# Attention weights of batches 3 to 7 transposed through DRAM and VectorE instead of TensorE, in a pooled-attention and FFN kernel

## The chip, the cores and the metric

The kernel runs on one NeuronCore of a Trainium2 chip. A core has TensorE (in the profile PE for matmuls, PEld for the loads of their stationary operand), VectorE (DVE), ScalarE (ACT), GpSimd (POOL), SyncE (SP, which only issues DMAs here) and 16 DMA engines. Each engine has its own queue and works through it in order; semaphores tie them together. The metric is the device time of one execution in microseconds (us).

## The reference

```python
# B, H, S, D = 8, 8, 576, 64; Sp = 72 pooled keys
k_p = k.reshape(B, H, Sp, 8, D).mean(axis=3)
v_p = v.reshape(B, H, Sp, 8, D).mean(axis=3)
scores = matmul(q, k_p.transpose(0, 1, 3, 2)) / sqrt(D)
attn = exp(scores - scores.max(-1, keepdims=True))
attn = attn / (attn.sum(-1, keepdims=True) + 1e-09)
x = matmul(attn, v_p).transpose(0, 2, 1, 3).reshape(B * S, H * D)   # 4608 x 512
h = x @ w_in                                                         # 512 x 2048
out = maximum(0.01 * h, h) @ w_out                                   # 2048 x 512
```

All is float32. The FFN matmuls and attention times V are done in a rounded format (F32R) with each operand split into a high and a low part, and three products hi*hi, hi*lo, lo*hi.

## The kernel before

**FFN.** The 4608 rows of x are worked through in nine chunks of 512, the first one in two halves, so there are ten stretches. In a stretch, each of 16 blocks of d_ff has an `m1` (12 matmuls into `ph`, lines 677 to 679, then Prelu, the cast `gh` and the remainder `gl`) and, two blocks behind, an `m2` (12 matmuls into the four accumulators `acc`, lines 701 to 703). `ph` has two PSUM banks.

**Attention.** A batch has five tiles of q rows: four of 128 and one of 64, in two pieces (three in batches 0 and 2). Its heads go in two groups of four (g = 0, 1), so a batch has ten units of tile and group. A unit goes through these steps:
- `q_unit`: q comes from DRAM in 16 small DMAs with its 32x32 blocks in place, and VectorE transposes the blocks (line 380); from batch 1 on.
- `s_unit` (`sa`): two matmuls give the scores `pss` (line 409), VectorE takes the negated maximum (417), ScalarE the exponentials with their sums (419).
- `norm_unit` (`sb`): VectorE adds 1e-9 and takes the reciprocal (430, 431), GpSimd writes `at`, the normalised weights, in two products (433, 437): keys 0 to 63 of the heads in pairs, and the last 8 keys of each head four times over.
- `p_unit` (`pu`): TensorE transposes `at` in three 128-column matmuls into the PSUM tile `pp` (line 458); ScalarE copies `pT` hi and rem from it (460, 461), VectorE writes the low parts (464, 468).
- `av_unit` (`au`), once for each piece and group: 8 matmuls `pa` (483 to 486) from `pT` and the pooled V, then x hi and lo (500, 501). There is one set of `pT` for both groups.

**Order.** TensorE's order is written out by hand: a list of attention steps (`line_up`) is spread evenly over the beats of a stretch, two beats per `m1` or `m2`, and reaches its end four beats before the stretch does. A stretch takes the pieces that make the next chunk. The order on the other engines comes from a planner that simulates the program; it is fixed at run time. From batch 1 on, `pss`, `pp`, `pa`, `pk`, `pv` share two PSUM banks. The pool `three` has three buffers for `at`, `outs` three for `o`.

Of the kernel before, what the change touches and what calls it, by code (L numbers as in the profile page):

```python
# [10 lines left out]
F32 = mybir.dt.float32  # L11
# [4 lines left out]
ALU = mybir.AluOpType  # L16
# [8 lines left out]
def tile_pooled_attention_ffn(  # L25
# [9 lines left out]
    nc = tc.nc  # L35

    P = 128
# [3 lines left out]
    MAIN = 64  # L41
    REM = SP - MAIN
# [13 lines left out]
    PIECES = [  # L56
        [[(0, 128), (128, 128)], [(256, 128), (384, 128)], [(512, 64)]],
        WHOLE,
        [[(0, 128), (128, 128)], [(256, 128)], [(384, 128), (512, 64)]],
        [[(0, 128), (128, 128), (256, 64)], [(320, 128), (448, 128)]],  # L60
        WHOLE,
        WHOLE, WHOLE, WHOLE,
    ]
# [4 lines left out]
    )  # L68
    TAIL_STEPS = "pu40 au20 pu41 au21"
    SPLIT = 8  # L70
    KSCALE = 1.0 / (POOL * 8.0)

# [133 lines left out]
    def bank(b, name):  # L206
        nonlocal turn
        pool, tag = banks[turn % len(banks)] if b == 0 else banks[0]
        turn += 1
        return pool.tile([P, NK, P], F32, tag=tag, name=name)  # L210
# [216 lines left out]
    def norm_unit(b, t, g, e, sm):  # L427
        n = tiles[b][t][1]
        eng = nc.vector if b == 0 and t in NORM_DVE else nc.gpsimd
        nc.vector.tensor_scalar_add(sm[:n], sm[:n], 1e-9)  # L430
        nc.vector.reciprocal(sm[:n], sm[:n])  # L431
        at = wide(b, t, g, "at", [3, P]) if wide_at(b, t, "at") else three.tile([P, 3, P], F32, tag="at", name=f"at{b}_{t}_{g}")
        eng.tensor_tensor(  # L433
            at[:n, 0:2, :].rearrange("a i (h s) -> a (i h) s", h=2), e[:n, :, 0:MAIN],
            sm[:n].unsqueeze(2).broadcast_to([n, 4, MAIN]), op=ALU.mult,
        )
        ins = eng.tensor_tensor(
            at[:n, 2, :].rearrange("a (h c s) -> a h c s", h=4, c=4),
            e[:n, :, MAIN:].unsqueeze(2).broadcast_to([n, 4, 4, REM]),
            sm[:n].unsqueeze(2).unsqueeze(3).broadcast_to([n, 4, 4, REM]), op=ALU.mult,  # L440
        )
        if b == 0:
            anchor[eng] = ins
        return at

    def piece_tiles(b, j, g):
        if b > 0 or g == 0 or j == 2:
            return pT
        return {
            part: spare(10 - n // 2, n % 2, t.shape, F32R, f"pT_{part}{b}_{j}_{g}")  # L450
            for n, (part, t) in enumerate(pT.items())
        }

    def p_unit(b, t, g, at, pc, o):
        n = tiles[b][t][1]
        pp = bank(b, f"pp{b}_{t}_{g}")
        for i in range(3):
            nc.tensor.transpose(pp[:, i, :n], at[:n, i, :], ident[:n, :n])  # L458
        rem = pc["rem"][:, o : o + n]
        nc.scalar.copy(pc["hi"][:, :, o : o + n], pp[:, 0:2, :n])  # L460
        ins = nc.scalar.copy(rem, pp[:, 2, :n])
        if b == 0:
            anchor["act"] = ins
        nc.vector.tensor_tensor(
            pc["lo"][:, :, o : o + n], pp[:, 0:2, :n], pc["hi"][:, :, o : o + n].bitcast(F32),
            op=ALU.subtract,
        )
        nc.vector.scalar_tensor_tensor(
            rem, pp[:, 2, :n], m_lo, rem.bitcast(F32), op0=ALU.mult, op1=ALU.subtract
        )  # L470
# [59 lines left out]
    def attention(b):  # L530

        st = {}
        where = [(j, sum(n for _, n in piece[:i]))
                 for j, piece in enumerate(PIECES[b]) for i in range(len(piece))]

        def loads():
            (start_k, st["k"]), (start_v, st["v"]) = load_k(b), load_v(b)
            start_k()
            q_of[b, 0] = load_q(b, 0)
            q_of[b, 1] = load_q(b, 1)  # L540
            start_v()
            for t in range(2, 5):
                q_of[b, t] = load_q(b, t)

        def loads1():
            (start_k, st["k"]), (start_v, st["v"]) = load_k(b), load_v(b)
            start_k()
            start_v()

        def lk():  # L550
            st["ks"] = load_k(b)[1]() if b > 1 else st["k"]()

        def lv():
            st["vs"] = load_v(b)[1]() if b > 1 else st["v"]()

        def ku():
            place_k(b, *st["ks"])

        def vu():
            place_v(b, *st["vs"])  # L560

        def qu(t):
            def f():
                st["qT", t] = q_unit(b, t, q_of[b, t])
                after = every.index((b, t)) + 2
                if after < len(every) and every[after] not in q_of:
                    q_of[every[after]] = load_q(*every[after])
            return f

        def sa(t, g):  # L570
            def f():
                st["e", t, g] = s_unit(b, t, g, st["qT", t])
            return f

        def sb(t, g):
            def f():
                st["at", t, g] = norm_unit(b, t, g, *st["e", t, g])
            return f

        def pu(t, g):  # L580
            def f():
                j, o = where[t]
                if (j, g) not in st:
                    st[j, g] = piece_tiles(b, j, g)
                p_unit(b, t, g, st["at", t, g], st[j, g], o)
            return f

        def au(j, g):
            def f():
                av_unit(b, j, g, st[j, g])  # L590
            return f

        return {
            "loads": loads1 if b else loads, "lk": lk, "lv": lv, "ku": ku, "vu": vu,
            **{f"q{t}": qu(t) for t in range(len(where))},
            **{f"{n}{t}{g}": u(t, g) for n, u in (("sa", sa), ("sb", sb), ("pu", pu))
               for t in range(len(where)) for g in range(2)},
            **{f"au{j}{g}": au(j, g) for j in range(len(PIECES[b])) for g in range(2)},
        }

    def line_up(pieces):

        flat = [(b, j, t) for b, j in pieces for t in range(len(tiles[b]))
                if tiles[b][t] in PIECES[b][j]]
        out = []

        def add(b, u):
            out.append((b, u))

        fresh = {}  # L610
        for n, (b, j, t) in enumerate(flat):
            nxt = flat[n + 1] if n + 1 < len(flat) else None
            first = n == 0 or flat[n - 1][:2] != (b, j)
            last = nxt is None or nxt[:2] != (b, j)
            if n == 0:
                if t == 0:
                    add(b, "ku")
                add(b, f"q{t}")
            if (b, t) not in fresh:
                add(b, f"sa{t}0")  # L620
            if not first:
                add(b, f"pu{t - 1}0")
            if (b, t) not in fresh:
                add(b, f"sb{t}0")
            if nxt:
                add(nxt[0], f"q{nxt[2]}")
            add(b, f"sa{t}1")
            if n == 0 and t == 0:
                add(b, "vu")
            if last:  # L630
                if not first:
                    add(b, f"pu{t}0")
                    add(b, f"sb{t}1")
                else:
                    add(b, f"sb{t}1")
                    if nxt and nxt[0] == b:
                        add(b, f"sa{nxt[2]}0")
                        fresh[nxt[0], nxt[2]] = 1
                    add(b, f"pu{t}0")
                if nxt and nxt[0] == b and (nxt[0], nxt[2]) not in fresh:  # L640
                    add(b, f"sa{nxt[2]}0")
                    fresh[nxt[0], nxt[2]] = 1
                if nxt and nxt[0] != b:
                    add(nxt[0], "ku")
                add(b, f"au{j}0")
                mine = [x[2] for x in flat if x[:2] == (b, j)]
                for i, x in enumerate(mine):
                    add(b, f"pu{x}1")
                    if i == 0 and nxt and nxt[0] == b:
                        add(b, f"sb{nxt[2]}0")  # L650
                add(b, f"au{j}1")
                if nxt and nxt[0] != b:
                    add(nxt[0], "vu")
            else:
                add(b, f"sb{t}1")
        return out


# [123 lines left out]
            beside[2 if c == 2 else c].append((b, j))  # L782
    units = []
    for n, pieces in enumerate(beside):
        us = [att[b][u] for b, u in line_up(pieces)]
        if n == 0:
            us = [att[0][u] for u in TAIL_STEPS.split()] + us
        if n == 2:
            us = [fetch] + us
        units.append(us)  # L790
# [76 lines left out]
```

## Time and profile before

| | us |
|---|---|
| median of 3 runs | 999.76 (999.34 to 1000.57) |
| profiled execution, as a run | 996.95 |
| its span, first to last instruction | 995.2 |
| PE busy | 938.7 |
| VectorE, ScalarE, GpSimd busy | 387.7, 411.5, 179.1 |

In the profile, a group row names line, engine, operation, `out<-in`, shapes and count, then total busy time and the mean of one in ns, then the idle time ahead of the group and what ended it. A timeline row is the start in us, the length in us, engine, line, operation and count; in brackets the engine's idle time before it and its releaser. The mean granted clock of TensorE is 0.977 of full speed; it is below 1 mostly in the first 100 us, in which weights and the first batch arrive. DMA engines are busy under a third of the time after that. Records of matmuls overlap, since they are pipelined; the time that one takes in the stream is read from start to start.

### The profile page before, as it was taken

The numbers are of one execution on the slowest core, as the hardware profiler recorded it, in microseconds if no ns is written. First come the engines' busy times: TensorE is split into PE (matmuls) and PEld (weight loads), VectorE is DVE, ScalarE is ACT, GpSimd is POOL, SyncE is SP. The second block draws the span as 40 slices with busy tenths as digits, with TensorE's granted clock in tenths as the row PEclk, the third lists the DMA queues.
The fourth block names the chain that finished last, engine by engine and source line by source line (L and its number), as shares of the span: only waits on it lengthen the run. The fifth ranks groups of instructions, "written<-read, shape, count | busy, mean of one in ns | idle before, by whom it ended". The sixth has DMA issues, their size and how long they took to land.

```text
span 995.2 us, 13059 instructions
## 1 busy us (share of the span) xinstructions
PE 938.7 (94%) x4396; PEld 768.8 (77%) x4396; DVE 387.7 (39%) x937; ACT 411.5 (41%) x1351; POOL 179.1 (18%) x292
## 2 busy tenths in 40 slices
PE   4558989999999999999999999999999999999998
PEld 4446778888877778878887888788877888788886
DVE  5979749423432342333233433243333422221111
ACT  4757757334433243434343434344433433322212
POOL 3611200311106630133013401230110100100000
PEclk9679999999999999999999999999999999999999
DMA  9765422311124420222022201210110010001001
GB/s 243 193 188 165 126 54 81 90 48 49 18 53 123 109 38 8 57 58 53 10 60 63 53 13 53 48 29 15 54 20 2 6 43 1 1 1 42 1 1 43
DMA packets 105667, 57.50 MB, mean 58 GB/s; under 512 B 80512, under 2 KB 88704, under 8 KB 105600
## 3 DMA queue, kind: packets, MB, share of 16 engines
q1 hardware_dynamic: 105600, 56.67, 21.7%
q8 instruction: 35, 0.57, 0.2%
q14 instruction: 32, 0.26, 0.1%
HBM read 46.14 MB, written 10.49 MB: 57 GB/s over the span
## 4 chain that ended last, share of the span: by engine, by line
PE 86%; DMA 5%; ACT 3%; SPq 3%; DVE 2%; issue 1%; POOL 0%; DVEq 0%; ACTq 0%
PE ph L677 13%; PE acc L701 13%; PE ph L679 13%; PE ph L678 13%; PE acc L703 13%; PE acc L702 13%; PE pss L409 3%; PE pp L458 2%; DMA q<-in_q_dram 2%; DMA w_bits<-in_moe_w_in_dram 1%; DMA v0raw<-in_v_dram 1%; SPq L331 1%; PE pa L483 1%; PE pa L484 1%; SPq L240 1%
## 5 line engine op out<-in xcount | busy, mean ns | idle before, releaser
L677 PE MATMUL ph<-xh,w 128*128 128x512 f32 x576 | 235.1, 408 | 0.0
L701 PE MATMUL acc<-w,gh 128*128 128x512 f32 x576 | 231.2, 401 | 0.0
L679 PE MATMUL ph<-xh,w 128*128 128x512 f32 x576 | 226.7, 394 | 0.0
L678 PE MATMUL ph<-xl,w 128*128 128x512 f32 x576 | 226.5, 393 | 0.0
L703 PE MATMUL acc<-w,gl 128*128 128x512 f32 x576 | 225.2, 391 | 0.0
L702 PE MATMUL acc<-w,gh 128*128 128x512 f32 x576 | 225.0, 391 | 0.0
L686 DVE TENSOR_TENSOR gl<-ph,gh 128x512 fp32r<-128x512 f32 x144 | 99.3, 689 | 258.7 <-ACT gh L685 258.1
L682 ACT ACTIVATE ph<-ph 128x512 f32<-128x512 f32 x144 | 84.2, 585 | 272.9 <-PE ph L679 272.8
L419 ACT ACTIVATE e<-pss,red 128x72 f32<-128x72 f32 (+1 forms) x320 | 98.1, 320 | 123.2 <-DVE red L417 123.1
L433 POOL TENSOR_TENSOR at<-e,red 128x256 f32<-128x256 f32 (+1 forms) x76 | 48.1, 633 | 531.5 <-DVE red L431 270.7
L679 PEld LDWEIGHTS ph<-xh,w 128*128 128x128 f32 x576 | 109.0, 189 | 24.0
L703 PEld LDWEIGHTS acc<-w,gl 128*128 128x128 f32 x576 | 108.2, 188 | 23.5
L677 PEld LDWEIGHTS ph<-xh,w 128*128 128x128 f32 x576 | 109.1, 189 | 22.2 <-issue 1.4
L701 PEld LDWEIGHTS acc<-w,gh 128*128 128x128 f32 x576 | 108.2, 188 | 22.4 <-issue 1.6
L678 PEld LDWEIGHTS ph<-xl,w 128*128 128x128 f32 x576 | 109.2, 190 | 19.6
L702 PEld LDWEIGHTS acc<-w,gh 128*128 128x128 f32 x576 | 108.3, 188 | 20.3
L685 ACT CAST gh<-ph 128x512 fp32r<-128x512 f32 x144 | 85.2, 592 | 3.4
L417 DVE TENSOR_REDUCE red<-pss 128x4 f32<-128x288 f32 (+1 forms) x80 | 36.1, 453 | 83.8 <-PE pss L409 83.0
L419 ACT ACTIVATION_READ_ACCUMULATOR e<-pss,red 128x1 f32 (+1 forms) x320 | 65.3, 204 | 0.0
L409 PEld LDWEIGHTS pss<-kT,qT 128*128 128x128 f32 (+1 forms) x320 | 48.9, 190 | 19.4 <-ACT qT L386 4.8
L409 PE MATMUL pss<-kT,qT 128*128 128x144 f32 (+1 forms) x320 | 55.8, 303 | 8.4 <-ACT qT L386 4.0
L458 PE MATMUL pp<-ident,at 128*128 128x128 f32 (+1 forms) x240 | 40.6, 282 | 19.4 <-POOL at L433 9.2
(94 smaller groups left out, 804.9 us busy)
## 6 DMA issues: line engine op xcount, KB each, us to landing
out_dram<-o SPq DMA_DIRECT2D x35, 256.0 KB
w_bits<-in_moe_w_in_dram SPq DMA_DIRECT2D x16, 512.0 KB
w_bits<-in_moe_w_out_dram SPq DMA_DIRECT2D x16, 512.0 KB
q<-in_q_dram SPq DMA_DIRECT2D x448, 16.0 KB
k0raw<-in_k_dram SPq DMA_DIRECT2D x16, 256.0 KB
k1raw<-in_k_dram SPq DMA_DIRECT2D x16, 256.0 KB
v0raw<-in_v_dram SPq DMA_DIRECT2D x16, 256.0 KB
v1raw<-in_v_dram SPq DMA_DIRECT2D x16, 256.0 KB
```

Of the source, the lines that this page charges most:

```text
L409: nc.tensor.matmul(sc[:n, 2 * SP * i : 2 * SP * (i + 1)], qT[:, p, :n], kT[:, p, :, :].rearrange("d i s -> d (i s)"), start=True, stop=True,)
L419: ins = nc.scalar.activation(e[:n, h, :], scv[:n, h, :], AF.Exp, bias=mx[:n, h : h + 1], accum_out=sm[:n, h : h + 1],)
L458: nc.tensor.transpose(pp[:, i, :n], at[:n, i, :], ident[:n, :n])
L677: nc.tensor.matmul(ph, w[:, 0, ks], xh[kk], start=kk == 0, stop=False)
L678: nc.tensor.matmul(ph, w[:, 0, ks], xl[kk], start=False, stop=False)
L679: nc.tensor.matmul(ph, w[:, 1, ks], xh[kk], start=False, stop=kk == NK - 1)
L682: nc.scalar.activation(ph, ph, AF.Prelu, alpha=0.01)
L685: casts.append(nc.scalar.copy(gh, ph))
L686: nc.vector.tensor_tensor(gl, ph, gh.bitcast(F32), op=ALU.subtract)
L701: nc.tensor.matmul(a, gh[:, r], hi, start=first, stop=False)
L702: nc.tensor.matmul(a, gh[:, r], lo, start=False, stop=False)
L703: nc.tensor.matmul(a, gl[:, r], hi, start=False, stop=last)
```

## The change

For batches 3 to 7 (`VIA = 3`) the transposes on TensorE are taken out. `norm_via` writes `at` in another layout (for each block of 32 columns its three parts side by side: three GpSimd products, of 128 columns each) and stores it in a DRAM tile `rows`, 1536 bytes for each of its rows. `fetch_via` loads it back in four DMAs, one for each block of 32 keys: 32 partitions get the 384-byte piece of that block from every row. So each 32x32 block lies in the partitions where its transpose belongs, and one VectorE transpose makes `pp`, now a tile in SBUF. `blocks` takes its buffers from the same three as `at`, `pp` from the three of `o`. The copies from `pp` to `pT` stay as they are. For these batches `line_up_via` lays out the steps: `pu` of a whole piece after the next tile's first group, `au` of the first group and the second `pu` a group later, `au` of the second group another group later; and at the end of a stretch one empty step between them.

```diff
+    VIA = 3
...
+    def norm_via(b, t, g, e, sm):
+        n = tiles[b][t][1]
+        nc.vector.tensor_scalar_add(sm[:n], sm[:n], 1e-9)
+        nc.vector.reciprocal(sm[:n], sm[:n])
+        at = three.tile([P, 4, 3, 32], F32, tag="at", name=f"at{b}_{t}_{g}")
+        for i in range(2):
+            nc.gpsimd.tensor_tensor(
+                at[:n, :, i, :].rearrange("a (h f) j -> a h f j", h=2),
+                e[:n, 2 * i : 2 * i + 2, 0:MAIN].rearrange("a h (f j) -> a h f j", f=2),
+                sm[:n, 2 * i : 2 * i + 2].unsqueeze(2).unsqueeze(3).broadcast_to([n, 2, 2, 32]),
+                op=ALU.mult,
+            )
+        nc.gpsimd.tensor_tensor(
+            at[:n, :, 2, :].rearrange("a h (c s) -> a h c s", c=4),
+            e[:n, :, MAIN:].unsqueeze(2).broadcast_to([n, 4, 4, REM]),
+            sm[:n].unsqueeze(2).unsqueeze(3).broadcast_to([n, 4, 4, REM]), op=ALU.mult,
+        )
+        rows = dram.tile([P, 4, 96], F32, name=f"rows{b}_{t}_{g}")
+        nc.sync.dma_start(rows[:n], at[:n].rearrange("a b i j -> a b (i j)"))
+        return rows
+
+    def fetch_via(b, t, g, rows):
+        n = tiles[b][t][1]
+        m = n // 32
+        blocks = three.tile([P, 4, 3, 32], F32, tag="at", name=f"blocks{b}_{t}_{g}")
+        for x in range(4):
+            nc.sync.dma_start(
+                blocks[32 * x : 32 * x + 32, :m].rearrange("s a i j -> s a (i j)"),
+                rows[:n, x, :].rearrange("(a s) x -> s a x", s=32),
+            )
+        pp = five.tile([P, 3, P], F32, tag="o", name=f"pp{b}_{t}_{g}")
+        nc.vector.transpose(
+            pp[:, :, :n].rearrange("k i (a s) -> k a i s", s=32), blocks[:, :m]
+        )
+        return pp
...
     def p_unit(b, t, g, at, pc, o):
         n = tiles[b][t][1]
-        pp = bank(b, f"pp{b}_{t}_{g}")
-        for i in range(3):
-            nc.tensor.transpose(pp[:, i, :n], at[:n, i, :], ident[:n, :n])
+        if b >= VIA:
+            pp = fetch_via(b, t, g, at)
+        else:
+            pp = bank(b, f"pp{b}_{t}_{g}")
+            for i in range(3):
+                nc.tensor.transpose(pp[:, i, :n], at[:n, i, :], ident[:n, :n])
...
+    def line_up_via(pieces):
...
+            if nxt is None or nxt[:2] != (b, j):
+                mine = [x[2] for x in flat if x[:2] == (b, j)]
+                later(n + 1, 0, [(b, f"pu{x}0") for x in mine])
+                later(n + 1, 1, [(b, f"au{j}0"), *((b, f"pu{x}1") for x in mine)])
+                later(n + 2, 0, [(b, f"au{j}1")])
+                if nxt and nxt[0] != b:
+                    later(n + 2, 0, [(nxt[0], "vu")])
...
+        for key in sorted(ends):
+            out += [None, *ends[key]]
+        return out
```

TensorE at the end of the stretch that makes chunk 6, from the last scores of the piece (batch 6, tile 1, second group: `pss6_1_1`) to its `pa`; `ph` and `acc` are the FFN's, and the names end in numbers of the program. Before:

```order
L409 MATMUL pss6_1_1_6342<-kT_103,qT6_1_6225 128x144 x2
L677 MATMUL ph5_13_6352<-xh5_0_5092,w0_13_1754 128x512
...
L679 MATMUL ph5_13_6352<-xh5_3_5095,w0_13_1754 128x512
L458 MATMUL pp6_1_0_6370<-ident_87,at6_1_0_6333 128x128 x3
L701 MATMUL acc6_0_5716<-w1_11_1663,gh5_11_6268 128x512
...
L703 MATMUL acc6_3_5738<-w1_11_1663,gl5_11_6269 128x512
L483 MATMUL pa6_0_0_6395<-pT_hi_111,v_hi_104 128x256
```

And with the change:

```order
L410 MATMUL pss6_1_1_6493<-kT_103,qT6_1_6121 128x144 x2
L754 MATMUL ph5_12_6503<-xh5_0_5288,w0_12_1672 128x512
...
L780 MATMUL acc6_3_5888<-w1_10_1577,gl5_10_6401 128x512
L754 MATMUL ph5_13_6552<-xh5_0_5288,w0_13_1754 128x512
...
L756 MATMUL ph5_13_6552<-xh5_3_5291,w0_13_1754 128x512
...
L780 MATMUL acc6_1_5870<-w1_11_1663,gl5_11_6463 128x512
L525 MATMUL pa6_0_0_6587<-pT_hi_111,v_hi_104 128x256
```

The group of transposes between them is gone, and 42 FFN matmuls (12 + 12 + 12 + 6) stand where 24 stood: the scores come earlier relative to `pa`.

SP's queue at the same place; `q` are q loads for the next tiles, `vremraw` a load for the next batch's V. Before:

```order
L258 DMA vremraw7_6048<-in_v_dram 64x1x512
L331 DMA q6_4_6545<-in_q_dram 32x2x32 x16
L331 DMA q7_0_6631<-in_q_dram 32x4x32 x16
L734 DMA out_0_dram<-o6_0_6604 128x512
L734 DMA out_0_dram<-o6_1_6611 128x512
```

And with the change, stores (`rows`) and fetches (`blocks`) among them:

```order
L475 DMA blocks5_4_1_6382<-rows5_4_1_6068 32x2x96 x4
L332 DMA q6_4_6749<-in_q_dram 32x2x32 x13
L466 DMA rows6_1_0_6432<-at6_1_0_6428 128x384
L259 DMA vremraw7_6228<-in_v_dram 64x1x512
L332 DMA q7_0_6802<-in_q_dram 32x4x32 x3
L475 DMA blocks6_0_0_6541<-rows6_0_0_6152 32x4x96 x2
L466 DMA rows6_1_1_6516<-at6_1_1_6512 128x384
L475 DMA blocks6_0_0_6541<-rows6_0_0_6152 32x4x96 x2
L475 DMA blocks6_1_0_6559<-rows6_1_0_6432 32x4x96 x4
L475 DMA blocks6_0_1_6616<-rows6_0_1_6307 32x4x96 x4
L475 DMA blocks6_1_1_6638<-rows6_1_1_6516 32x4x96 x4
L332 DMA q7_0_6802<-in_q_dram 32x4x32 x13
```

The fetches that the first `pa` needs are `blocks6_0_0` and `blocks6_1_0`; two and four of them stand behind the store of `at6_1_1`.

More of the change, by code (lines that the diff above doesn't have):

```diff
@@ L576, in f @@
             def f():
-                st["at", t, g] = norm_unit(b, t, g, *st["e", t, g])
+                norm = norm_via if b >= VIA else norm_unit
+                st["at", t, g] = norm(b, t, g, *st["e", t, g])
             return f
@@ L655, in line_up, with later @@
                 add(b, f"sb{t}1")
+        return out
+    def line_up_via(pieces):
+        flat = [(b, j, t) for b, j in pieces for t in range(len(tiles[b]))
+                if tiles[b][t] in PIECES[b][j]]
+        out, ends = [], {}
+        def later(n, g, steps):
+            ends.setdefault((n, g), []).extend(steps)
+        for n, (b, j, t) in enumerate(flat):
+            nxt = flat[n + 1] if n + 1 < len(flat) else None
+            if t == 0:
+                out.append((b, "ku"))
+            if n == 0:
+                out.append((b, f"q{t}"))
+            if nxt is None or nxt[:2] != (b, j):
[5 more added lines that the diff above has]
+                    later(n + 2, 0, [(nxt[0], "vu")])
+            for g in range(2):
+                out.append((b, f"sa{t}{g}"))
+                if g == 0 and nxt:
+                    out.append((nxt[0], f"q{nxt[2]}"))
+                out.append((b, f"sb{t}{g}"))
+                if g == 1 and n == 0 and t == 0:
+                    out.append((b, "vu"))
+                out += ends.pop((n, g), [])
+        for key in sorted(ends):
+            out += [None, *ends[key]]
         return out
@@ L784, in tile_pooled_attention_ffn @@
     for n, pieces in enumerate(beside):
-        us = [att[b][u] for b, u in line_up(pieces)]
+        us = [att[b][u] for b, u in line_up([x for x in pieces if x[0] < VIA])]
+        us += [
+            att[x[0]][x[1]] if x else lambda: None
+            for x in line_up_via([x for x in pieces if x[0] >= VIA])
+        ]
         if n == 0:
```

## The prediction

> **What bounds the kernel now.** I read the page's first part, then the chain of waits, then the busy time by stretches, then who waits on the engine that these name.
>
> ```profile
> PE 938.7 (94%) x4396; PEld 768.8 (77%) x4396; DVE 387.7 (39%) x937; ACT 411.5 (41%) x1351; POOL 179.1 (18%) x292
> PE 86%; DMA 5%; ACT 3%; SPq 3%; DVE 2%; issue 1%; POOL 0%; DVEq 0%; ACTq 0%
> 500.00:600.00 100.00, 100.00 (x482) 81.90 (x481) 35.86 (x95) 40.87 (x145) 22.21 (x36) 1.00 0.20 47
> 395.00:890.00 495.00, 493.51 (x2352) 405.00 (x2352) 164.64 (x424) 192.82 (x681) 79.29 (x138) 1.00 0.13 32
> PE pv L366 <- DVE xl L501: 1.5, 2, 0.7
> ```
>
> The first two lines are the page's: TensorE carries 86% of the chain that ends last. The next two are stretches (length, then busy time of PE, PEld, DVE, ACT and POOL, granted clock, DMA share, GB/s). From 395 to 890 us, where most of the attention of batches 3 to 7 runs between the FFN matmuls, PE is busy 493.5 of 495 us at full granted clock, and the other engines a third of the time or less. The last line is the only wait on PE in that stretch: 1.5 us in all. So here the span is the sum of what PE is given; a matmul taken out shortens it by the room it takes in PE's stream, as long as nothing new makes PE wait.
>
> **What is removed from PE.** A matmul's record overlaps its neighbours' (0.39 us long, 0.23 apart), so its room is read from starts, not from durations.
>
> ```profile
> 612.99 0.39 PE L677 MATMUL ph<-xh,w 128*128 128x512 f32 x1
> 613.22 0.39 PE L678 MATMUL ph<-xl,w 128*128 128x512 f32 x1
> 613.45 0.40 PE L679 MATMUL ph<-xh,w 128*128 128x512 f32 x1
> 613.68 0.49 PE L458 MATMUL pp<-ident,at 128*128 128x128 f32 x3
> 613.93 0.48 PE L677 MATMUL ph<-xh,w 128*128 128x512 f32 x1
> 614.24 0.39 PE L678 MATMUL ph<-xl,w 128*128 128x512 f32 x1
> ...
> 754.61 0.39 PE L703 MATMUL acc<-w,gl 128*128 128x512 f32 x1
> 754.92 0.40 PE L458 MATMUL pp<-ident,at 64*128 64x64 f32 x3
> 755.25 0.50 PE L677 MATMUL ph<-xh,w 128*128 128x512 f32 x1
> 755.59 0.39 PE L678 MATMUL ph<-xl,w 128*128 128x512 f32 x1
> ```
>
> From 613.45 to 614.24 are 0.79 us for two FFN matmuls, 2 x 0.23, and one group of three transposes: the group takes 0.33 us. The 64-row group takes 755.59 - 754.61 - 0.46 = 0.52 us, more, since PE stops on both sides of it. Five batches have four full tiles and one of 64 rows, each for two groups of heads: 40 x 0.33 + 10 x 0.52 = **18.4 us** off PE.
>
> In the Trainium skill, TensorE: Matmul & The Clock Gate, Part 4: PE-mode transpose, a transpose in a kernel's context is given as about 275 ns. By that, 150 of them would give 41 us. The starts in this trace leave 0.11 us for each, and the sum goes by them. VectorE: DVE Perf Modes, Rules for kernel authors, advises TensorE for a 128x128 transpose because VectorE's spans 32x32 blocks only, which speaks against the detour; here DMAs place the blocks, and what that may cost is the first rival.
>
> **What is added, and where it hides.**
>
> ```profile
> L380 DVE STREAM_TRANSPOSE qT<-q 128x512 f32<-128x512 f32 x28 | 19.8, 706 | 4.9 <-DMA q<-in_q_dram 4.9
> L380 DVE STREAM_TRANSPOSE qT<-q 128x256 f32<-128x256 f32 x7 | 3.1, 438 | 0.0
> L433 POOL TENSOR_TENSOR at<-e,red 128x256 f32<-128x256 f32 x60 | 37.4, 623 | 446.5 <-DVE red L431 261.1 <-ACT ph L682 131.3 <-ACT pT_rem L461 36.8
> L437 POOL TENSOR_TENSOR at<-e,red 128x128 f32<-128x128 f32 x60 | 24.9, 415 | 0.0
> L464 DVE TENSOR_TENSOR pT_lo<-pp,pT_hi 128x256 fp32r<-128x256 f32 x64 | 27.0, 421 | 53.3 <-ACT pT_rem L461 52.9
> 517.04 7.42 SPq L331 DMA_DIRECT2D q<-in_q_dram  x16
> 74.17 2.81 DMA q<-in_q_dram
> 95.09 1.59 DMA q<-in_q_dram
> 989.41 1.99 DMA out_dram<-o
> ```
>
> VectorE gets 40 transposes of 384 columns, midway between 438 and 706 ns, so 0.57 us, and 10 of 192, under 0.44: at most 27 us on the 165 busy of 495. GpSimd's 256-column product becomes two of 128, 2 x 415 instead of 623 ns: 0.2 us x 50 = 10 us on 79. The copies out of `pp` stay, and read SBUF where they read PSUM; I take their durations as they are, and the bound from both sides is the spread of 0.1 us or so between like rows, which the same cover hides. These engines are idle for more than half of the stretch; what they gain in work costs nothing until they are late for PE. Without that cover it would be 27 + 10 = 37 us, twice the gain.
>
> SP gets 250 issues (one store and four fetches in each of 50 units) at 7.42 / 16 = 0.46 us, 116 us on some 500. Beside its 16 issues per q tile that is room enough on average. What matters is the order: SP waits at a store until GpSimd has written `at`, with q loads, k and v loads and out stores behind it, and at a fetch for the store's landing. No row of before shows a 192 KB store or a 48 KB fetch; the nearest landings, the last three rows, give 1.6 to 2.8 us, and I take 2.0, the 256 KB store's, since both new transfers are of its order or smaller.
>
> **Where PE could meet the new path late.** In the middle of a stretch the first `pa` comes a whole tile later. It is tight where the last piece of a stretch ends: there `pa` needs `pT` from the fetches that stand behind the last tile's store. In the stretch shown in the order of instructions above (batch 6, tile 1, second group) PE has 42 FFN matmuls between `pss` and `pa`, in the other five 48 or more. The way up to the store is seen at the same kind of tile now:
>
> ```profile
> 671.51 0.65 PE L409 MATMUL pss<-kT,qT 128*128 128x144 f32 x4
> ...
> 672.20 0.46 DVE L417 TENSOR_REDUCE red<-pss 128x4 f32<-128x288 f32 x1 [0.97 <-PE pss L409]
> ...
> 672.75 0.32 ACT L419 ACTIVATE e<-pss,red 128x72 f32<-128x72 f32 x1 [2.25 <-DVE red L417]
> ...
> 674.31 0.18 DVE L431 RECIPROCAL red<-red 128x4 f32<-128x4 f32 x1
> ...
> 674.66 0.61 POOL L433 TENSOR_TENSOR at<-e,red 128x256 f32<-128x256 f32 x1 [3.70 <-DVE red L431]
> 675.23 0.40 POOL L437 TENSOR_TENSOR at<-e,red 128x128 f32<-128x128 f32 x1
> ```
>
> `at` is written 675.63 - 671.51 = 4.1 us after `pss` starts, 4.3 with the split product. Then SP: the store 0.46, and the sixth fetch behind it, the last one that the first `pa` needs, is issued 5 x 0.46 later, at 7.1 us; it lands 2.0 after its issue; VectorE's transpose 0.57, `pT_hi` and `pT_rem` on ScalarE 0.7 (their rows run 0.38 and 0.28), `pT_lo` 0.42: **10.8 us**. PE is there after `pss` at 0.39 and 42 x 0.23 = 10.1 us: 0.7 us late. With 48 matmuls it is there at 11.4, and with 54 at 12.8: not late. `pa` of the second group has 30 matmuls more, 6.9 us, for eight more fetches, 3.7 us: not late. VectorE waiting at a transpose holds back the `gl` behind it, which frees the bank that PE writes 36 matmuls, 8.3 us, after that block's last.
>
> Two things can add to that. ScalarE or VectorE may be held by another wait just there, as ScalarE was once by batch 4's `vremparts`, without a wait on PE then:
>
> ```profile
> 452.01 0.26 ACT L357 ACTIVATE vremparts<-vremsum 64x64 fp32r<-64x64 f32 x1 [7.07 <-POOL vremsum L234]
> 329.25 0.40 PE L366 MATMUL pv<-vremparts,spread 32*128 32x64 f32 x2 [1.57 <-DVE xl L501]
> 331.00:334.20 3.20, 3.20 (x11) 2.71 (x10) 0.46 (x1) 1.21 (x8) 1.50 (x3) 0.50 0.60 189
> ```
>
> And a pause of PE can bring a slow spell: after the 1.57 us of the second row the granted clock was 0.50 for 3.2 us (third row), 1.6 us lost. So new waits cost from 0 up to 2 + 1.6 us at each of six ends, 22 us. I take **2.5 us** in all, near the low end, because only one of six is late by the sum, and 1.5 us is what PE waits in this stretch now.
>
> **Sum.** 995.2 - 18.4 + 2.5 = 979.3 us of span. The profiled execution took 996.95 us as a run, the median of the runs shown is 999.76: the same 15.9 off gives 983.9, and I say **984 us**.
>
> **Rivals.**
> *The store's way becomes the bound (slower).* Place: SP's queue at the six ends. If a store or a fetch stands behind a whole q tile there, 16 issues, 7.4 us, each end waits some 6.5 us and draws a slow spell of 1.6: 6 x 8.1 = 49 against 18.4 gives 1030. It decides from 18.4 / 6 = 3.1 us per end, or 1.5 with the slow spell. For it: 13 q loads stand just ahead of tile 1's first store. Against: SP is through them when `at` is there, and its issues fill under half its time.
> *Ends late by about 2 us without slow spells:* 6 x 2 = 12, 999.8 - 18.4 + 12 = 993. For it: the landing may be 2.8 us, and VectorE's queue has a q transpose in front. Against: only one end is late by the sum.
> *PE's room is not released* (the FFN matmuls are paced by `gh` and `gl`, and the transposes sat in slots that stay empty): 1000. Against: 0.23 us from start to start without a wait, and two thirds of ScalarE and VectorE free.
> *The groups cost what their records last.* 33.9 us for 192 full and 6.7 for 48 half transposes (their group rows below) would be 21.2 + 4.2 = 25.4 for these 150: 977 with the same 2.5. Against: records overlap.
>
> ```profile
> L458 PE MATMUL pp<-ident,at 128*128 128x128 f32 x192 | 33.9, 292 | 7.7 <-DVE at L433 5.0 <-DVE x_tail L504 1.8 <-DVE xl L501 0.8
> L458 PE MATMUL pp<-ident,at 64*128 64x64 f32 x48 | 6.7, 244 | 11.7 <-POOL at L433 9.2 <-DVE x_tail L504 1.5 <-issue 0.7
> ```
>
> **Chances.** Forecast 0.66, its own range 979 to 989; late ends 0.17; PE's room not released 0.05; the longer records 0.04; SP the bound 0.08. The range of 977 to 996 takes in the forecast, the late ends and the bounds of the waits (0 to some 15 us), and leaves out about 0.15. A measurement here tells about 0.2%, 2 us, from no change. Faster by more: 0.66 + 0.04 + 0.15 of the late ends = 0.85. Within: 0.05 + 0.02 = 0.07. Slower: 0.08.
>
> **What the changed profile would show.** PE's groups: no `pp` for batches 3 to 7, 150 matmuls fewer. PE at 98% or more of the stretch up to the last `pa`, which ends some 16 us earlier; the waits on PE there under 5 us. If `pa` or its weight loads appear as waiting for ScalarE's `pT_hi` or VectorE's `pT_lo` by 10 us and more, behind transposes that wait for DMA, the slack was mis-sized and the second rival holds; granted clock of 0.5 past 400 us adds the slow spells. If SP shows stores waiting behind q issues, it is the first. If PE has the matmuls fewer but its FFN matmuls stand further than 0.23 us apart, the third.

## The result and the profile after

| | before | after |
|---|---|---|
| median | 999.83 us (999.34 to 1000.57) | 982.62 us (981.33 to 985.1) |
| profiled execution, as a run | 996.95 us | 983.37 us |
| its span | 995.2 us | 981.6 us |

The ratio of the two kernels is 0.985, 95% interval 0.9824 to 0.9875. The forecast was 984 us, range 977 to 996.

First the profile's first part for the changed kernel (busy time, share and count of each engine), then the longer of the two stretches whose rows of before the prediction shows (length, then busy time of PE, PEld, DVE, ACT and POOL, granted clock, DMA share, GB/s):

```profile
PE 922.0 (94%) x4246; PEld 757.0 (77%) x4246; DVE 410.2 (42%) x987; ACT 414.5 (42%) x1351; POOL 185.4 (19%) x342
```

```profile
395.00:890.00 495.00, 492.39 (x2290) 405.91 (x2289) 187.86 (x472) 200.37 (x689) 85.51 (x182) 1.00 0.25 64
```

150 matmuls fewer, PE still busy for 492.4 of 495 us, and every other engine busy for some two fifths of it or less: the bound is the same. Over the whole execution VectorE gained 22.5 us of work, GpSimd 6.3 and ScalarE 3.0, and none of it shows in PE's share.

To see where the time went I need two points at which both kernels have done the same work. The 804th FFN matmul stands just before batch 3's first part that differs; the 3456th is the last. Both as rows of the timeline of PE (start in us, length), of before and of after:

```profile
296.50 0.39 PE L679 MATMUL ph<-xh,w 128*128 128x512 f32 x1
...
990.16 0.39 PE L703 MATMUL acc<-w,gl 128*128 128x512 f32 x1
```

```profile
299.11 0.39 PE L756 MATMUL ph<-xh,w 128*128 128x512 f32 x1
...
976.47 0.39 PE L780 MATMUL acc<-w,gl 128*128 128x512 f32 x1
```

Between the two points before takes 693.7 us and after 677.4: **16.3 us less**. The first 300 us, which the change does not touch, took 2.6 us longer in this execution of after; that is why the two spans differ by only 13.6. In the ten profiled kernels of this study that have batches 0 to 2 unchanged, this first part ends between 296.4 and 300.6 us, so it says nothing of the change, and from here on I compare profiles from the 804th matmul.

The room of a group of attention matmuls is what it adds between the FFN matmuls around it: from the last FFN start before it to the second one after it, less two spacings of 0.2275 us. Summed over all groups between the two points (`pk` with `pkr`, and `pv`, are the few matmuls that put a batch's pooled K and V in place):

| groups on PE | before | after | difference |
|---|---|---|---|
| `pp`, 128 rows | 42: 14.38 | 2: 0.68 | -13.70 |
| `pp`, 64 rows | 12: 6.34 | 2: 1.06 | -5.28 |
| `pa` | 22: 24.15 | 22: 33.21 | +9.06 |
| `pv` | 5: 7.39 | 5: 3.68 | -3.71 |
| `pss` | 52: 30.65 | 52: 29.78 | -0.87 |
| `pk`, `pkr` | 5: 4.23 | 5: 4.38 | +0.15 |
| half-clock spacings between FFN matmuls outside these rooms | 0.75 | 0.28 | -0.47 |

That makes -14.8 of the -16.3 us. The other 1.5 us is in the ordinary spacings: outside the rooms and the spells the FFN matmuls start 0.2285 us apart on average before and 0.2279 after. It goes with the transposes: the kernel below that has them back is at 0.2286 again, and the other nine without them are at 0.2278 to 0.2279. So the groups cost PE some 20.5 us, the 19.0 of the first two rows and 1.5 in the spacings behind them.

The new waits are in the list of waits on PE from 299 us on (engine and line, what it waited for, us in total, times, longest), of after and of before:

```profile
PE pa L525 <- ACT pT_hi L502: 5.2, 3, 4.0
PE pa L525 <- ACT e L420: 0.6, 1, 0.6
PE pa L526 <- DVE pT_lo L506: 0.5, 1, 0.5
```

```profile
PE pv L366 <- DVE xl L501: 3.0, 3, 1.6
```

PE now waits for `pT_hi` at `pa`, and no longer at `pv` (a 0.6 us wait at `pa` is left out of the list of before). Four `pa` groups cost 0.6 to 1.5 us more than the median one of after, and a fifth, the first `pa` of batch 3's three-tile piece at the end of its stretch, 5.5 us. This is that place in the timeline of after: GpSimd's last products of two units and SP's queue, then VectorE, then PE (in brackets idle time and releaser), and last a window for the granted clock:

```profile
357.71 0.40 POOL L460 TENSOR_TENSOR at<-e,red 128x128 f32<-128x128 f32 x1
...
361.06 0.39 POOL L460 TENSOR_TENSOR at<-e,red 64x128 f32<-64x128 f32 x1
...
358.13 0.34 SPq L466 DMA_DIRECT2D rows<-at  x1
358.52 2.83 SPq L332 DMA_DIRECT2D q<-in_q_dram  x6
361.45 0.51 SPq L466 DMA_DIRECT2D rows<-at  x1
362.00 3.66 SPq L332 DMA_DIRECT2D q<-in_q_dram  x5
365.76 1.32 SPq L475 DMA_DIRECT2D blocks<-rows  x3
367.18 0.49 SPq L466 DMA_DIRECT2D rows<-at  x1
367.72 8.36 SPq L475 DMA_DIRECT2D blocks<-rows  x17
```

```profile
373.65 0.38 DVE L480 STREAM_TRANSPOSE pp<-blocks 128x192 f32<-128x192 f32 x1 [0.17 <-DMA blocks<-rows]
```

```profile
374.41 0.63 PE L525 MATMUL pa<-pT_hi,v_hi 128*128 128x320 f32 x1 [3.98 <-ACT pT_hi L502]
```

```profile
374.40:377.90 3.50, 3.49 (x11) 3.25 (x12) 2.35 (x6) 2.33 (x7) 0.00 (x0) 0.52 0.40 91
```

SP issues the store at 358.13, as soon as GpSimd has written `at` (357.71 + 0.40), and then q loads and stores in turn. The last unit's `at` is written at 361.45, but its store goes out at 367.18, 5.7 us later, behind q loads and the first three fetches. The first fetch goes out at 365.76, behind all q loads, and the twelfth, on which the first `pa` depends (three tiles, four fetches each, nine of them behind the last store), at 367.72 + 8 x 0.49 = 371.6. PE waits 3.98 us, and then the granted clock is 0.52 for 3.5 us.

### The profile page after: what moved, and what is told of

Read it like the earlier page. It is cut to its first block, busy times and chain, and to the rows that moved or that the text cites. A ratio compares the mean times of both kernels' runs of the same rounds, so it can differ in the third digit from the quotient of the medians.

```text
span 981.6 us, 13210 instructions
## 1 busy us (share of the span) xinstructions
PE 922.0 (94%) x4246; PEld 757.0 (77%) x4246; DVE 410.2 (42%) x987; ACT 414.5 (42%) x1351; POOL 185.4 (19%) x342
## 5 line engine op out<-in xcount | busy, mean ns | idle before, releaser
L756 PEld LDWEIGHTS ph<-xh,w 128*128 128x128 f32 x576 | 109.2, 190 | 23.7
L454 POOL TENSOR_TENSOR at<-e,red 128x128 f32<-128x128 f32 (+1 forms) x100 | 37.8, 398 | 318.3 <-DVE red L451 216.5
L502 ACT CAST pT_hi<-pp 128x256 fp32r<-128x256 f32 (+1 forms) x80 | 30.0, 378 | 81.0 <-DVE pp L480 67.3
```

The source lines that it names most:

```text
L454: nc.gpsimd.tensor_tensor(at[:n, :, i, :].rearrange("a (h f) j -> a h f j", h=2), e[:n, 2 * i : 2 * i + 2, 0:MAIN].rearrange("a h (f j) -> ...
L756: nc.tensor.matmul(ph, w[:, 1, ks], xh[kk], start=False, stop=kk == NK - 1)
```

## The experiments

All ratios are to the kernel before, run beside each experiment. "From 804" is the time between the two points above in the profile; `pa` and `pv` are the sums of the table. In the last two kernels batch 2 changes as well, and "from 804" leaves out what that does before the 804th matmul.

| kernel | median, us | ratio (95%) | from 804 | `pa` | `pv` |
|---|---|---|---|---|---|
| before | 999.83 | 1 | 693.7 | 24.2 | 7.4 |
| after | 982.62 | 0.985 (0.9824 to 0.9875) | 677.4 | 33.2 | 3.7 |
| transposes back on PE | 1004.25 | 1.0056 (1.0037 to 1.0075) | 698.0 | 28.9 | 3.6 |
| old order, no transposes, no way | 983.53 | 0.9844 (0.9817 to 0.9871) | 678.4 | 23.7 | 11.3 |
| new order, no transposes, no way | 980.91 | 0.9801 (0.9756 to 0.9846) | 675.1 | 23.3 | 7.3 |
| fetches of the first store | 984.25 | 0.9861 (0.9845 to 0.9877) | 679.6 | 33.1 | 3.8 |
| eight fetches per unit | 1029.48 | 1.0318 (1.0296 to 1.0339) | 723.6 | 72.3 | 3.6 |
| q loads behind fetches | 976.63 | 0.9782 (0.9755 to 0.981) | 671.0 | 26.5 | 3.7 |
| stores from GpSimd | 977.78 | 0.9803 (0.9778 to 0.9828) | 673.3 | 28.0 | 3.7 |
| both of these | 975.28 | 0.9773 (0.9757 to 0.9788) | 671.0 | 26.5 | 3.7 |
| q loads behind fetches, from batch 2 | 980.53 | 0.9828 (0.9811 to 0.9845) | 679.0 | 34.4 | 4.4 |
| both, from batch 2 | 977.02 | 0.9778 (0.9757 to 0.9798) | 674.9 | 25.7 | 4.4 |

### Is it PE's room?

My theory: the gain is the room of the transposes in PE's stream. The rivals: it comes from the new order of steps, or the room is not released. Two kernels separate these.

**Transposes back on PE**, with a result that nothing reads:

```diff
             pp = fetch_via(b, t, g, at)
+            idle = bank(b, f"idle{b}_{t}_{g}")
+            for i in range(3):
+                nc.tensor.transpose(idle[:, i, :n], ident[:n, :], ident[:n, :n])
```

> The changed kernel with three more transposes on TensorE in each of the 50 units of batches 3 to 7, of the constant identity into a PSUM bank that nothing reads; the way through DRAM stays and the result is the same. Theory (the gain is PE's room): the groups take 40 x 0.34 + 10 x 0.53 = 19 us of PE again; the waits at the ends of stretches may shrink by a microsecond or two because PE comes there later. So 982.6 + 19 - 2 = 1000 us (997 to 1003), about the kernel before: the new way itself costs next to nothing. Rival (the new order of the attention steps made the gain, not the room): 983 us.

1004.25 us, a little past the upper end: 20.6 us above after from 804 on, and the same 0.0206 in the ratios. The groups of lines in the profile have the 150 matmuls:

```profile
L499 PE MATMUL idle<-ident 128*128 128x128 f32 (+1 forms) x150 | 23.7, 266 | 2.8 <-DVE xl L546 2.8
```

Their records add up to 23.7 us, their room from starts to 16.9 + 5.3 = 22.2, of which 2.8 are waits (the row's idle time). The theory holds, the order as the cause of the gain falls. "The way itself costs next to nothing" does not hold: with all transposes on PE again this kernel is 0.0056, some 5.6 us, above the kernel before. The way through DRAM and its order of steps together have a price; the largest part of it is in the `pa` groups, 28.9 us against 24.2 before.

**Old order, without transposes and without the way:**

```diff
-        pp = bank(b, f"pp{b}_{t}_{g}")
-        for i in range(3):
-            nc.tensor.transpose(pp[:, i, :n], at[:n, i, :], ident[:n, :n])
+        if b >= 3:
+            pp = ident.unsqueeze(1).broadcast_to([P, 3, P])
+        else:
+            ...
```

> The kernel before, with its order of steps, but without the 150 transposes and without the way through DRAM: for batches 3 to 7 pT is copied from the constant identity, so the attention weights do not enter the output and only the time means something. Theory: the groups' room, 19.3 us, goes and nothing new waits: 999.8 - 19.3 = 980.5 us (978 to 983). Then the way through DRAM in the changed kernel costs 2 us net. Rival (PE's room is not released, since the FFN's own pace holds): 999 to 1000 us.

983.53 us, just past the upper end. The room is released (the rival falls), but 15.3 us of it arrive and not 19 or more: with PE earlier, `pv` comes before VectorE's `v_rem`. The waits on PE from 300 us on, and two windows in which the half-clock spells behind them lie:

```profile
PE pv L366 <- DVE v_rem L369: 5.8, 4, 2.4
PE pv L366 <- DVE xl L504: 0.8, 1, 0.8
```

```profile
334.00:339.00 5.00, 5.00 (x17) 4.12 (x17) 1.97 (x6) 1.31 (x8) 2.38 (x4) 0.66 0.46 131
655.00:659.40 4.40, 4.40 (x16) 3.69 (x15) 1.29 (x5) 1.30 (x9) 1.47 (x3) 0.61 0.06 21
```

So part of the room is given back wherever the next input is not ready. That suggested that the changed kernel's new order is what spared it the `pv` waits, and a third kernel tested it.

**New order, without transposes and without the way:**

```diff
         if b >= VIA:
-            pp = fetch_via(b, t, g, at)
+            pp = ident.unsqueeze(1).broadcast_to([P, 3, P])
...
-        rows = dram.tile([P, 4, 96], F32, name=f"rows{b}_{t}_{g}")
-        nc.sync.dma_start(rows[:n], at[:n].rearrange("a b i j -> a b (i j)"))
-        return rows
+        return at
```

> The changed kernel with its new order of steps, but without the store, the fetches and VectorE's transposes: for batches 3 to 7 pT is copied from the constant identity, so the attention weights do not enter the output and only the time means something. It differs from the run with the old order and no transposes by the order of the steps, and from the changed kernel by the way through DRAM alone. Theory (the new order takes away the waits of PE at pv and the half-clock spell behind them; the way costs the late first pa's and their spell, some 10 us): 982.6 - 10 = 972 to 974 us. Rival (the new order itself brings pa too early and is what the late pa's come from): 981 to 984 us.

980.91 us, 7 us above the theory's range and at the edge of the rival's; the interval reaches from 975 to 984. The theory's half on the way holds: without it the late `pa` are gone (23.3 us for the groups, 24.2 before the change). With that the rival's mechanism falls, since the new order alone brings no `pa` too early. The theory's half on the order falls: the waits at `pv` are back, in the new order too.

```profile
PE pv L367 <- DVE v_rem L370: 2.7, 2, 1.4
PE pss L410 <- DVE kT L347: 1.4, 1, 1.4
```

```profile
559.00:562.40 3.40, 3.40 (x11) 2.81 (x11) 1.28 (x4) 0.01 (x1) 1.48 (x3) 0.54 0.70 186
661.00:666.10 5.10, 5.10 (x18) 4.11 (x19) 1.84 (x7) 0.26 (x2) 1.49 (x3) 0.67 0.07 22
```

The `pv` waits are for VectorE, whose order the planner lays out anew for every variant; that this order decides them is my reading, and I did not try it by itself. What the changed kernel saved at `pv`, 3.7 us and the spell behind it, is therefore real in its profile, but I can't tie it to the new list of steps.

### What makes the first `pa` late?

Three causes were possible: the store's landing ahead of a fetch, SP's queue, or the engines behind the fetch.

**Fetches of the first store:**

```diff
-                rows[:n, x, :].rearrange("(a s) x -> s a x", s=32),
+                first_rows[0][:n, x, :].rearrange("(a s) x -> s a x", s=32),
```

> The changed kernel, but every fetch reads the first store's tile in DRAM, so that no fetch waits for its own store to land; stores, issues and order stay. The attention weights of batches 3 to 7 are then those of one unit, and only the time means something. Theory (the fetches of the first pa are issued late because of the queue; their stores landed long before): 981 to 984 us, with the first pa of batch 3's last piece late as before. Rival (the way through DRAM, a store's landing of 2 us ahead of a fetch, is what PE waits for): 974 to 978 us.

984.25 us, no different from after, and the same `pa` waits as long:

```profile
374.62 0.63 PE L528 MATMUL pa<-pT_hi,v_hi 128*128 128x320 f32 x1 [3.96 <-ACT pT_hi L505]
```

The stores' landing is not what PE waits for. The theory holds.

**Eight fetches of 16 partitions instead of four of 32**, the same bytes:

```diff
         for x in range(4):
-            nc.sync.dma_start(
-                blocks[32 * x : 32 * x + 32, :m].rearrange("s a i j -> s a (i j)"),
-                rows[:n, x, :].rearrange("(a s) x -> s a x", s=32),
-            )
+            for y in range(2):
+                r = 32 * x + 16 * y
+                nc.sync.dma_start(
+                    blocks[r : r + 16, :m].rearrange("s a i j -> s a (i j)"),
+                    rows[:n, x, :].rearrange("(a s) x -> s a x", s=32)[16 * y : 16 * y + 16],
+                )
```

> The changed kernel with each fetch split in two of 16 partitions, so that 200 issues more go through SP; bytes and order stay. Theory (SP's issues are what makes the first pa of a stretch's end late): six to twelve issues of 0.46 us more ahead of it, 2.8 to 5.5 us at each of the four ends that are already late, less where there is slack: 12 to 20 us in all, 994 to 1003 us. Rival (the time from issue to landing decides, and the queue has room): 983 to 986 us.

1029.48 us, 47 more than after and far above the theory's own 20. SP's queue and the wait at batch 3's end, and the waits on PE from 342 to 880 us:

```profile
366.43 21.39 SPq L477 DMA_DIRECT2D blocks<-rows  x45
...
378.87 0.64 PE L527 MATMUL pa<-pT_hi,v_hi 128*128 128x320 f32 x1 [9.83 <-ACT pT_hi L504]
```

```profile
PE pa L527 <- ACT pT_hi L504: 36.9, 8, 9.8
```

An issue takes 21.39 / 45 = 0.475 us. At batch 3's end the first `pa` needs twelve fetches, now 24: 12 x 0.475 = 5.7 us more, and the wait grew by 9.83 - 3.98 = 5.85. So the mechanism and its rate hold. What was mis-sized is the number of places: eight `pa` wait for `pT_hi` instead of three, the longest 9.8 us, among them places that had slack before, and the pauses draw half-clock spells (6.2 us in the spacings outside the rooms, 0.3 in after). The `pa` groups, 39.1 us more, and these spacings make up 45 of the 46.2 us from 804 on. At this doubling SP's queue makes eight `pa` late, and the kernel is slower than before.

**Later q loads queued behind the fetches:**

```diff
-                    q_of[every[after]] = load_q(*every[after])
+                    with tc.issue_after(via_last[0].ins) if via_last[0] else nullcontext():
+                        q_of[every[after]] = load_q(*every[after])
```

where `via_last` holds the last fetch that the program has laid out.

> The changed kernel, but loads of later q tiles are queued on SP behind the fetches that are already there in the program. Theory (at batch 3's end 16 q loads stand ahead of the fetches in SP's queue, and the 4.0 us wait of the first pa there and its slow spell come from that): that wait goes, 5 us off, 977 to 978 us; the other ends, with less in front, gain little. Rival (the wait comes from the stores' landing or from VectorE): 982 to 983 us. Against both: if the q tile of the next stretch then comes late for its scores, a new wait stands there and the time is 983 to 986.

**Stores issued by GpSimd:**

```diff
-        nc.sync.dma_start(rows[:n], at[:n].rearrange("a b i j -> a b (i j)"))
+        nc.gpsimd.dma_start(rows[:n], at[:n].rearrange("a b i j -> a b (i j)"))
```

> The changed kernel, with the stores issued by GpSimd instead of SP; the fetches stay on SP. Theory (it is the fetches behind the q loads that are late, not the store): batch 3's end still waits, since 16 q loads stand ahead of the first fetch there as before; 981 to 984 us. Rival (the store's place in SP's queue is what makes the ends late): 5 us and more off, 975 to 978 us. A second rival: issuing takes GpSimd's own time, holds its products back and makes at late: 985 to 990 us.

976.63 and 977.78 us. SP's queue at batch 3's end with the q loads behind the fetches, and then, with the stores from GpSimd, SP's queue, GpSimd's last store and PE:

```profile
353.60 7.71 SPq L468 DMA_DIRECT2D rows<-at  x3
361.62 1.27 SPq L477 DMA_DIRECT2D blocks<-rows  x3
```

```profile
351.75 8.95 SPq L332 DMA_DIRECT2D q<-in_q_dram  x19
360.88 11.18 SPq L475 DMA_DIRECT2D blocks<-rows  x21
...
361.45 0.59 POOL L466 DMA_DIRECT2D rows<-at  x1 [0.30 <-POOL at L460]
...
370.08 0.41 PE L525 MATMUL pa<-pT_hi,v_hi 128*128 128x320 f32 x1 [0.72 <-ACT pT_hi L502]
```

Counted from the 804th matmul of each kernel, the first fetch goes out after 66.7 us in after (365.76 - 299.1), 61.5 with the q loads behind (their 804th is at 300.1) and 64.4 with the stores from GpSimd (296.5). The first kernel confirms the theory: that `pa` no longer waits, and 6.3 us are gained from 804 on, a little more than the expected 5. The second kernel has the rival's number and goes against the theory of its expectation. All 16 q loads of the next tile are still ahead of the fetches, and yet the fetches start 2.3 us earlier and the wait falls from 3.98 to 0.72 us (1.6 of this because PE comes later, after a longer wait at `pkr`: 5.9 us for the `pk` groups against 4.4). So it is not the q loads as such: in the changed kernel SP stands at a store until GpSimd has written `at`, the q loads pile up behind it, and they go out when the fetches should. SP's own waits in after from 350 to 370 us show it (us in total, times, longest):

```profile
SPq L466 <- POOL at L460: 3.8, 2, 2.5
```

With the store out of the queue, SP issues the q loads while it would have stood still. By the medians this kernel's interval and after's just touch (0.9828 and 0.9824); from 804 on it is 4.1 us ahead.

The second rival, a GpSimd held up by issuing, did not show: a store takes 0.59 us there, and the products are in time.

**Both edits:**

> Both edits of SP's queue in one: the stores issued by GpSimd, and the later q loads behind the fetches. Theory (both cure the same thing, fetches behind q loads that pile up while SP waits for a store): no more than either alone, and of the late first pa's some 1 to 3 us are left, since GpSimd, ScalarE and VectorE still need their time there: 975 to 978 us. Rival (the two act at different places, and their gains add up, 6 and 5 us): 971 to 973 us.

975.28 us. The theory holds: the two cure the same wait and do not add up. Left are 2.0 us of waits at `pa` from 297 us on:

```profile
PE pa L527 <- ACT e L420: 1.6, 2, 1.1
...
PE pa L527 <- ACT pT_hi L504: 0.4, 1, 0.4
```

This version beats both kernels: 0.9773 of before, its interval clear of after's. Against the q loads alone, 0.9782, it can't be told apart.

### From batch 2 on

**VIA = 2 with the q loads behind the fetches**

```diff
-    VIA = 3
+    VIA = 2
```

> The changed kernel from batch 2 on instead of batch 3, with the later q loads behind the fetches. Theory: 8 more full groups of transposes and 2 more half ones leave PE, 8 x 0.34 + 2 x 0.53 = 3.8 us: 976.6 - 3.8 = 973 us (971 to 975). Rival (in batch 2 PE is not what sets the end, since its weights and k and v loads still fill SP's queue and the DMA engines there): 976 to 980 us.

980.53 us, half a microsecond past the rival's range and a ratio 0.0046 above that of the same edit from batch 3, although ten more groups are off PE. The wait has moved to the end of batch 2; the last fetch laid out ahead of these q loads belongs to an earlier stretch, so nothing holds them back (timeline, SP's queue, GpSimd, then PE):

```profile
314.00 7.20 SPq L332 DMA_DIRECT2D q<-in_q_dram  x15
...
314.62 0.40 POOL L462 TENSOR_TENSOR at<-e,red 128x128 f32<-128x128 f32 x1
...
321.29 0.38 SPq L468 DMA_DIRECT2D rows<-at  x1
...
327.81 0.47 PE L527 MATMUL pa<-pT_hi,v_hi 128*128 128x256 f32 x1 [4.54 <-ACT pT_hi L504]
```

`at` is written at 315.0 and its store goes out at 321.29, behind 15 q loads. Neither reading fits whole: the number is nearly the rival's, but most of the loss is one `pa` wait behind q loads, as at batch 3's end in after.

**VIA = 2 with both edits**

> From batch 2 on, with the stores issued by GpSimd and the later q loads behind the fetches. In the run from batch 2 with only the q loads moved, PE waited 4.5 us for the first pa at batch 2's end, where 15 q loads stood ahead of the store. Theory (that wait is the same one again, and what ate the 3.8 us of the ten groups): with the store out of SP's queue it goes, and 975.3 - 3.8 = 971.5 us (970 to 974). Rival (batch 2's groups stood where PE had time to spare, 48.4 of 50 us busy there, or the fetches behind the q loads are late anyway): 975 us and more.

977.02 us, not below the 975.28 from batch 3. That `pa` wait is gone, as the theory said, and the next input is late in its place:

```profile
307.25 0.71 POOL L229 TENSOR_TENSOR kremraw<-kremraw 64x256 f32<-64x256 f32 x1 [1.49 <-DMA kremraw<-in_k_dram]
...
310.56 0.37 PE L342 MATMUL pkr<-ident,kremsum 64*128 64x64 f32 x1 [4.07 <-POOL kremsum L235]
```

```profile
311.40:316.20 4.80, 4.80 (x15) 3.93 (x14) 0.46 (x1) 0.80 (x5) 3.06 (x4) 0.51 0.62 138
```

Batch 3's K, which GpSimd prepares from loads in the same SP queue, is 4 us late, and a spell at half clock follows. Some of it is GpSimd's own time: between the row above and the sum that `pkr` reads, at 310.04, it makes another unit's `at` (1.1 us) and issues its store (0.59), so here GpSimd's queue is part of what PE waits for. The 3.8 us of room in batch 2 are not to be had by this alone.

## Why the prediction was right, point by point

**The bound** was right: PE at 492.4 of 495 us after, the other engines' added work hidden. One reading was off without consequence: ScalarE's 192.8 of 495 us are 39%, not a third or less.

**What is removed** was right to a tenth: 18.4 us were read from two groups, 13.70 + 5.28 = 19.0 are gone in the rooms, and 1.5 more in the spacings behind them. With the groups put in again the time from 804 on rose by 20.6 us, their rooms by 22.2 (2.8 of them waits). The reading from starts also beats the two other prices: 25.4 by the records, and the estimate of 41 by the 275 ns of the Trainium skill (TensorE: Matmul & The Clock Gate, Part 4: PE-mode transpose). The trace agrees with that figure as the length of a record (292 ns on average at 128 rows) and not as room in the stream, where a group of three took 0.34 us at 128 rows and 0.53 at 64.

**What is added** hides, as said: VectorE's transposes took 0.58 and 0.38 us, against 0.57 and under 0.44, and GpSimd gained 6.3 us where 10 were taken. The landing was right too. These rows are the end of batch 6's tile 1, the place that the prediction worked out, after its `pss` at 665.98:

```profile
667.55 0.26 ACT L358 ACTIVATE vremparts<-vremsum 64x64 fp32r<-64x64 f32 x1 [3.94 <-POOL vremsum L235]
...
670.27 0.40 POOL L460 TENSOR_TENSOR at<-e,red 128x128 f32<-128x128 f32 x1
...
671.35 0.38 SPq L466 DMA_DIRECT2D rows<-at  x1
671.77 6.62 SPq L475 DMA_DIRECT2D blocks<-rows  x14
...
676.18 0.58 DVE L480 STREAM_TRANSPOSE pp<-blocks 128x384 f32<-128x384 f32 x1 [0.18 <-DMA blocks<-rows]
...
677.23 0.43 DVE L506 TENSOR_TENSOR pT_lo<-pp,pT_hi 128x256 fp32r<-128x256 f32 x1 [0.47 <-ACT pT_hi L502]
677.25 0.39 PE L525 MATMUL pa<-pT_hi,v_hi 128*128 128x256 f32 x1 [1.06 <-ACT pT_hi L502]
```

`at` is written 670.67 - 665.98 = 4.7 us after `pss` (4.3 predicted; `vremparts` held ScalarE, the risk that was named), the sixth fetch behind the store goes out at 671.77 + 5 x 0.47 = 674.1, or 8.1 (7.1 predicted), the transpose starts at 676.18, 2.1 us after that issue (2.0 taken), and `pT_lo` is done at 11.7 (10.8 predicted). PE waits 1.06 us where 0.7 was worked out, and the group costs 1.5 us more than a median one.

**The new waits** were mis-sized: the term of 2.5 us measured 9.1 in the `pa` groups. The step that failed is the sentence against the first rival, "SP is through them when `at` is there", and with it "With 48 matmuls ... not late". It was worked out for one of the six ends and carried over to the others. At batch 3's end SP was not through: it had stood at the stores before, the q loads came behind them, and the last store went out 5.7 us after its `at`. The `pa` there also needs nine fetches behind that store and not six; with these alone, 10.8 + 3 x 0.46 = 12.2 us against the 12.8 of its 54 matmuls, it would have been in time. 5.5 of the 9.1 us arose at this one end. The prediction's sign for this rival, a store that waits behind q issues, shows there; its other sign, waits on PE under 5 us, can't tell: they are 2.3 us in its stretch from 395 to 890 us, which begins behind batch 3's end at 374 us. So the rival of the store's way held at one place of six, with a slow spell of the size it named, and at eight `pa` groups once the issues were doubled: 1029 us.

**The sum** came out by luck, because a second term was missing: before's waits at `pv`, 3.7 us, and the half-clock spell behind one of them, 0.9 in `pss` and 0.5 outside the rooms, went away with the change. The prediction quoted both rows and counted neither as a gain. -19.0 - 1.5 + 9.1 - 3.7 - 0.9 - 0.5 = -16.5 (measured -16.3; `pk` adds 0.15) stands beside the predicted -15.9: the waits were 6.6 us more than taken, and 5.1 us at `pv` and its spell and 2.1 of the transposes offset that.

**The other rivals.** The room was released, as the kernels without transposes show, though 15 of 19 us arrived in the old order, since PE then waited at `pv`. Late ends of 2 us at each of six places did not occur; besides batch 3's, four `pa` groups cost 0.6 to 1.5 us, two of them ends (574 and 677 us) and two in the middle of a stretch (647 and 659), where the prediction had seen a whole tile of slack.

## What to carry to other kernels

Where PE is the bound, price work taken off it by starts in its stream, and then look for the next input that PE will reach too early: here some of each gain came back as a wait at `pa`, `pv` or `pkr`, with a slow spell behind it. A DMA that waits for a computed tile should not stand in an in-order queue ahead of loads that could already go, nor those loads ahead of what a bound engine needs next; moving the store to another engine's queue or the loads behind the fetches was worth another 5 or 7 us of 983, and both together 8 (0.9803, 0.9782 and 0.9773 against 0.985). Work out the deadline of a new path at each end that has one, not at one of them, and count the fetches that the first consumer needs.

## What the runs showed of the hardware

A pause of PE of 1.35 to 1.6 us was at times enough for a spell at half the granted clock (before: 1.57 us, then 0.50 for 3.2 us; the new order without the way has a 1.35 us wait at `pv` ahead of its second spell, first row), pauses of 4 us drew one each time (0.52 for 3.5 us, 0.51 for 4.8), and neither the 1.06 us above nor, in the kernel with the transposes put back, 1.53 us (second row) and 2.28 us ahead of the `pa` at 372.71 drew one.

```profile
660.55 0.41 PE L367 MATMUL pv<-vremparts,spread 32*128 32x64 f32 x2 [1.35 <-DVE v_rem L370]
```

```profile
448.21 0.55 PE L499 MATMUL idle<-ident 128*128 128x128 f32 x3 [1.53 <-DVE xl L546]
```

So a wait on PE of more than about 1.3 us may cost another 1.6 to 2.4 us, half of such a spell. What decides it can be read in part from the clock's records. From 300 us to the end of the FFN every spell lasts 3.41 us or two or three times that (3.41 in before from 330.79, 10.24 with eight fetches from 372.26), and within a trace the spells' ends lie whole multiples of 3.41 us apart. Cut on this grid into slices of 3.41 us, the twelve traces have 13 slices at full clock in which PE is idle for 1.9 us or more: a spell follows each. None follows a slice with 1.3 us or less; of the ten between, with 1.35 to 1.6, four drew one. The pause of 2.28 us lies across a boundary, 1.2 and 1.1 us in its two slices. What decides between 1.35 and 1.6, these runs don't show.

A group of three transposes of 64 rows takes more of PE than one of 128, 0.53 against 0.34 us, also when its input is a constant (the transposes put back), so it is not a wait for data. Finally, fetches of 48 KB (four of the 17 of 24) and ones half as large went through SP at 8.36 / 17 = 0.49 and 21.39 / 45 = 0.475 us each: in this queue the count mattered, not the bytes.
